# Weights narrowed in seven operations, w_in by halves, w_out inside the loop's first steps, a sign flip moved from GpSimd to ScalarE, and another order of loads, folds and DFT

## Chip, cores, metric

One core of a Trainium2 chip. The metric is the device time of one execution in microseconds (us), the median of several runs. "Span" is the profiled execution's time from the first to the last instruction; it is some 2 us below the run's time.

## The reference

```python
def reference(x, w_in, conv_w, w_out):      # x 8 x 3136 x 256; the weights come as float64
    x = np.fft.fft(np.fft.fft(x, axis=1), axis=2).real.astype(np.float32)
    h = np.maximum(x @ w_in, 0.0)           # w_in 256 x 1024
    conv = sum(conv_w[k] * shift(h, k) for k in range(3))   # along the sequence, zero-padded
    return (h / (1 + np.exp(-conv)) @ w_out).astype(np.float32)   # w_out 1024 x 256
```

The weights arrive as float64, and the kernel computes in fp32 (every matmul of the profile is f32): a "narrowing" takes the two 32-bit words of each float64 apart and builds an fp32 on VectorE.

## The kernel before

A prologue loads everything, narrows the weights, folds the first batch of x (sums and differences of mirrored rows, so that fewer DFT products are needed), multiplies the DFT of the feature axis into w_in (the tile G), and runs the DFT of batch 0 in nine parts. Then 256 steps follow, 32 for each of 8 batches. A step makes two products with G on TensorE, combines them on VectorE, convolves, takes a sigmoid, gates on GpSimd and VectorE, and multiplies by w_out. Folds and DFT of the next batch are "side" work of the steps.

The narrowing of a piece, ten VectorE operations:

```python
ts(out=fi, in0=hi, scalar1=20, scalar2=0x7FF, op0=lsr, op1=ALU.bitwise_and)
ts(out=fi, in0=fi, scalar1=896, scalar2=1151, op0=ALU.max, op1=ALU.min)
ts(out=fi, in0=fi, scalar1=23, scalar2=-0x40000000, op0=lsl, op1=ALU.bitwise_xor)
ts(out=gi, in0=hi, scalar1=-0x80000000, scalar2=None, op0=ALU.bitwise_and)
st(out=fi, in0=fi, scalar=0x7FFFFFFF, in1=gi, op0=ALU.bitwise_and, op1=ALU.bitwise_or)
ts(out=gi, in0=lo, scalar1=1, scalar2=None, op0=lsr)
st(out=g, in0=gi, scalar=2.0 ** -51, in1=f, op0=ALU.mult, op1=ALU.mult)
ts(out=hi_, in0=hi, scalar1=3, scalar2=0x7FFFF8, op0=lsl, op1=ALU.bitwise_and)
tt(out=fi, in0=fi, in1=hi_, op=ALU.bitwise_or)
tt(out=dst, in0=f, in1=g, op=ALU.add)
```

The DFT tables, loaded on SyncE's queue and mended on ScalarE (L198 and L207 to L212):

```python
def load_tables(par):                     # par 1: odd tables, par 0: even tables
    st = slice(2 * par, 2 * par + 2)
    to = tab[:, st].rearrange("p s q i -> p s (q i)")
    for i in range(2):
        nc.sync.dma_start(out=to[i:NP:2], in_=dft_seq[0:NP // 2, st, HQ * i:HQ * (i + 1)]...)  # 49 rows
    nc.sync.dma_start(out=tab[NP:KR, st, HQ - 1], ...)
    nc.sync.dma_start(out=tab[NP:KR, st, 0:HQ - 1], ...)

def mend_tables(par, half):
    row = tab[96:NP, 2 * par:2 * par + 2, HQ - 1]
    act(row, row, AF.Copy, scale=half[96:NP])
    if par:
        for i in range(2):
            for to, of, s in ((4, 3, -1.0), (5, 2, 1.0)):
                act(tab[0:KR, to, :, i:HO:2], tab[0:KR, of, :, i:HO:2], AF.Copy, scale=-s if i else s)
```

The loads of x: in h == 1, eight small "zero-row" loads (the rows that stand for row 0 of each quarter) go to eng2:

```python
def load_ops(b, h, eng, eng2):
    def plain():
        eng.dma_start(out=t[0:NP, 0:4], in_=...)
        if h == 1:
            for s in range(8):
                eng2.dma_start(out=t[NP:KR, s], in_=x[b:b + 1, r * Q4:r * Q4 + 1].to_broadcast([1, 2, D]))
...
for h in range(2):
    for f in load_ops(0, h, nc.sync, nc.scalar):
        f()
```

And the flip, the last operation on the row "er" before it goes out to DRAM and comes back to all partitions, where it seeds a batch's first products:

```python
nc.gpsimd.tensor_scalar(out=t[:, 3:NK:4], in0=t[:, 3:NK:4], scalar1=-1.0, scalar2=None, op0=ALU.mult)
nc.sync.dma_start(out=ed[b:b + 1, :], in_=t)
```

## Time and profile before

| | before |
|---|---|
| median of 3 runs | 1289.94 us |
| span, mean granted clock of TensorE | 1288.0 us, 0.987 |
| start of the first combine (end of the prologue) | 93.06 |
| batch 0 (32 steps) | 154.39 |
| batches 1 to 7, to the end | 1040.55 |

The last three rows sum to the span. They are read from VectorE's timeline: the combine is one VectorE instruction (L492, 512 times in the trace), two of them to a step, so every 64th marks a new batch. Each part of the change touches one of the three stages.

### The profile page before, as it was taken

The numbers are of one execution on the slowest core, as the hardware profiler recorded it, in microseconds if no ns is written. First come the engines' busy times: TensorE is split into PE (matmuls) and PEld (weight loads), VectorE is DVE, ScalarE is ACT, GpSimd is POOL, SyncE is SP. The second block draws the span as 40 slices with busy tenths as digits, with TensorE's granted clock in tenths as the row PEclk, the third lists the DMA queues.
The fourth block names the chain that finished last, engine by engine and source line by source line (L and its number), as shares of the span: only waits on it lengthen the run. The fifth ranks groups of instructions, "written<-read, shape, count | busy, mean of one in ns | idle before, by whom it ended". The sixth has DMA issues, their size and how long they took to land.

```text
span 1288.0 us, 15443 instructions
## 1 busy us (share of the span) xinstructions
PE 1198.0 (93%) x4914; PEld 898.6 (70%) x4914; DVE 1153.2 (90%) x1664; ACT 880.2 (68%) x1814; POOL 404.1 (31%) x507
## 2 busy tenths in 40 slices
PE   0758999999999999999999999999999999999998
PEld 0535677777677766777677776777677777777776
DVE  6869998998989988898899988998999878898996
ACT  0216766777668766777667776777767777777885
POOL 2414524241523334232513225141322213222222
PEclk9868999999999999999999999999999999999999
DMA  7701202020211102020202103020010001100101
GB/s 226 191 26 39 88 26 87 13 78 25 88 38 44 55 30 76 25 78 25 72 29 63 40 25 100 26 77 5 22 50 26 27 25 44 32 6 22 33 26 44
DMA packets 46842, 66.04 MB, mean 51 GB/s; under 512 B 5600, under 2 KB 35196, under 8 KB 46504
## 3 DMA queue, kind: packets, MB, share of 16 engines
q1 hardware_dynamic: 41012, 49.80, 12.5%
q0 software_dynamic: 5120, 12.85, 3.4%
q10 hardware_dynamic: 628, 2.40, 0.6%
q8 instruction: 38, 0.62, 0.2%
q14 instruction: 44, 0.36, 0.1%
HBM read 39.24 MB, written 25.74 MB: 50 GB/s over the span
## 4 chain that ended last, share of the span: by engine, by line
PE 69%; DVE 17%; issue 4%; ACT 4%; DMA 3%; POOL 2%; DVEq 0%; SPq 0%; ACTq 0%; POOLq 0%
PE po L89 43%; PE pb L89 10%; PE pa L89 9%; PE pd L89 7%; DVE g L504 4%; DVE h L492 2%; DVE g L518 2%; ACT nb L481 2%; DMA dm<-dft_dim_dram 1%; POOL er L319 1%; DVE w L174 1%; DVE xh L147 1%; DVE w L175 1%; DVE xh L158 1%; ACT g L510 1%
## 5 line engine op out<-in xcount | busy, mean ns | idle before, releaser
L89 PE MATMUL po<-wout,g 128*128 128x256 f32 (+2 forms) x3200 | 740.1, 381 | 26.6 <-DVE g L518 13.7
L89 PEld LDWEIGHTS po<-wout,g 128*128 128x128 f32 (+2 forms) x3200 | 597.3, 188 | 190.4 <-DVE g L518 43.4
L504 DVE SCALAR_TENSOR_TENSOR g<-h,cw,g 128x770 f32<-128x770 f32 (+2 forms) x512 | 556.9, 1088 | 11.0 <-ACT g L498 1.5
L517 POOL TENSOR_TENSOR g<-g,h 128x385 f32<-128x385 f32 (+1 forms) x256 | 239.5, 937 | 755.2 <-ACT g L510 571.7
L510 ACT ACTIVATE g<-g 128x385 f32<-128x385 f32 (+3 forms) x512 | 244.1, 527 | 187.6 <-DVE g L504 187.3
L481 ACT ACTIVATE nb<-pb 128x386 f32<-128x386 f32 (+4 forms) x512 | 225.5, 494 | 121.8 <-PE pb L89 120.9
L492 DVE CUSTOM_DVE_ANT_0 h<-pa,nb 128x386 f32<-128x386 f32 (+4 forms) x512 | 265.2, 560 | 15.8 <-PE pa L89 10.0
L498 ACT ACTIVATE g<-h,cw 128x770 f32<-128x770 f32 (+2 forms) x256 | 243.7, 952 | 0.0
L89 PE MATMUL pa<-pt,G 128*128 128x386 f32 (+2 forms) x512 | 213.7, 498 | 9.0 <-ACT pa L466 9.0
L89 PE MATMUL pb<-qt,G 127*128 127x386 f32 (+2 forms) x512 | 215.1, 501 | 4.7 <-ACT nb L481 4.7
L518 DVE TENSOR_TENSOR g<-g,h 128x385 f32<-128x385 f32 (+2 forms) x256 | 155.2, 606 | 5.3 <-ACT g L510 5.3
L466 ACT ACTIVATE pa<-eb,ge 128x386 f32<-128x386 f32 (+2 forms) x256 | 153.9, 601 | 8.2 <-DMA eb<-ed 8.0
L89 PEld LDWEIGHTS pa<-pt,G 128*128 128x128 f32 x512 | 97.4, 191 | 83.3 <-issue 19.8
L89 PE MATMUL pd<-tab,w 99*128 99x196 f32 (+2 forms) x448 | 118.6, 374 | 0.0
L89 PEld LDWEIGHTS pb<-qt,G 127*128 127x128 f32 x512 | 94.0, 191 | 32.0 <-ACT nb L481 7.9
L122 POOL DMA_INDIRECT xh<-in_x_dram,idx x64 | 88.0, 1374 | 16.4 <-issue 13.7
L89 PEld LDWEIGHTS pd<-tab,w 99*128 99x128 f32 (+1 forms) x448 | 83.2, 190 | 13.5
L534 ACT COPY os<-po 128x256 f32<-128x256 f32 (+2 forms) x200 | 60.1, 393 | 16.4 <-DMA out_dram<-os 8.6
L89 PE MATMUL po<-win,dm 128*128 128x512 f32 x8 | 6.5, 994 | 39.2 <-DMA dm<-dft_dim_dram 39.2
L147 DVE TENSOR_TENSOR xh<-xh 98x1020 f32<-98x1020 f32 (+1 forms) x32 | 43.0, 1353 | 0.0
L158 DVE TENSOR_TENSOR xh<-xh 98x1024 f32<-98x1024 f32 (+1 forms) x32 | 41.2, 1294 | 0.1
L89 PEld LDWEIGHTS po<-win,dm 128*128 128x128 f32 x8 | 2.5, 330 | 42.3 <-issue 41.3
(84 smaller groups left out, 373.0 us busy)
## 6 DMA issues: line engine op xcount, KB each, us to landing
out_dram<-os SPq DMA_DIRECT2D x184, 128.0 KB
xh<-in_x_dram SPq DMA_DIRECT2D x16, 784.0 KB
eb<-ed SPq DMA_DIRECT2D x16, 193.0 KB
tab<-dft_seq_dram SPq DMA_DIRECT2D x4, 601.8 KB
raw<-in_moe_w_in_dram ACTq DMA_DIRECT2D x2, 1024.0 KB
raw<-in_moe_w_out_dram SPq DMA_DIRECT2D x1, 2048.0 KB
eb<-ed SPq DMA_DIRECT2D x8, 209.0 KB
eb<-ed SPq DMA_DIRECT2D x8, 192.5 KB
```

Source lines behind the costliest of these rows:

```text
L89: nc.tensor.matmul(o, l, r, start=start, stop=stop, skip_group_check=True)
L122: nc.gpsimd.indirect_dma_start(out=xh[b, h][0:NP, 4 + m].rearrange("p q d -> p (q d)"), out_offset=None, in_=bass.AP(tensor=x.tensor, offs ...
L147: vt(a[:, :, :, 1:D], a[:, :, :, 1:D], r[:, :, :, D - 1:0:-1], op=ALU.add)
L466: act(pa[s][:, 0:n], eb[b, c], AF.Copy, scale=ge[:, f:f + 1])
L481: act(nb[s][:, i, cols], p[:, cols], AF.Copy, scale=-1.0 if i else 1.0)
L492: nc.vector._custom_dve(TENSOR_ADD_SAT, out=to, in0=a[:, cols], in1=c[:, i, cols], s0=BIG, s1=0.0)
L498: act(gs[s], hs[s][:, 0:n], AF.Copy, scale=cw[:, 0, s[2]:s[2] + 1])
L504: stt(out=g, in0=h[:, k:k + n], scalar=cw[:, k, f:f + 1], in1=g, op0=ALU.mult, op1=ALU.add)
L510: act(gs[s][:, c], gs[s][:, c], AF.Sigmoid)
L517: gt(g[:, m:n], g[:, m:n], h[:, m + 1:n + 1], op=ALU.mult)
L518: vt(g[:, 0:m], g[:, 0:m], h[:, 1:m + 1], op=ALU.mult)
L534: nc.scalar.copy(out=osb[0:m, j % 2], in_=pt[0:m, j % 2])
```

## The change

The intent: less VectorE work in the prologue (seven operations instead of ten; only half of w_in ahead of the folds, the other half between DFT parts; w_out in the steps 0 to 7), so that the DFT and the steps start earlier, and a GpSimd operation less in each batch. The diff, cut to its core:

```diff
-    def load_ops(b, h, eng, eng2):
+    def load_ops(b, h, eng):
...
-            if h == 1:
-                for s in range(8):
-                    r = s if s < 4 else (8 - s) % 4
-                    eng2.dma_start(out=t[NP:KR, s], in_=x[...].to_broadcast([1, 2, D]))
+        def zero():                      # five loads, on the queue of x
+            for s0, n, r, d in ((0, 4, 0, Q4), (4, 1, 0, Q4), (5, 1, 3, Q4), (6, 1, 2, Q4), (7, 1, 1, Q4)):
+                eng.dma_start(out=t[NP:KR, s0:s0 + n], in_=...)
...
-            return [pair(0), pair(2), both(4, ALU.add), both(6, ALU.subtract), evens, feats(0), feats(1)]
+            return [pair(0), pair(2), both(6, ALU.subtract), feats(1), both(4, ALU.add), evens, feats(0)]
...
-                nc.gpsimd.tensor_scalar(out=t[:, 3:NK:4], ..., scalar1=-1.0, ...)
+        def flip():
+            act(er[b][:, 3:NK:4], er[b][:, 3:NK:4], AF.Copy, scale=-1.0)
...
+        ts(out=d, in0=hi, scalar1=20, scalar2=0x7FF, op0=lsr, op1=ALU.bitwise_and)
+        ts(out=d, in0=d, scalar1=-896, scalar2=0, op0=ALU.add, op1=ALU.max)
+        ts(out=d, in0=d, scalar1=23, scalar2=None, op0=lsl)
+        stt(out=d, in0=hi, scalar=-0x80000000, in1=d, op0=ALU.bitwise_and, op1=ALU.bitwise_or)
+        ts(out=hi, in0=hi, scalar1=0xFFFFF, scalar2=0x100000, op0=ALU.bitwise_and, op1=ALU.bitwise_or)
+        stt(out=lof, in0=lo.bitcast(U32), scalar=2.0 ** -32, in1=hi, op0=ALU.mult, op1=ALU.add)
+        stt(out=dst, in0=lof, scalar=2.0 ** -20, in1=dst, op0=ALU.mult, op1=ALU.mult)
...
+    w_cv.load(nc.scalar)
+    w_in[0].load(nc.scalar, 0)
+    w_in[0].load(nc.sync, 1)
+    for h in range(2):
+        for f in load_ops(0, h, nc.sync):
+            f()
+    nc.scalar.dma_start(out=dm, in_=dft_dim[:, :, 0:2])
+    load_tables(1)
+    for t in range(2):
+        w_in[1].load(nc.sync, t)
+    load_tables(0)
...
+    for i, u in enumerate(us[j] for j in (0, 1, 4, 2, 3, 5, 6, 7, 8)):     # feature part third
+        u.matmuls(0, 1)
+        u.copy()
+        ...                                                                 # row at 1, flip and spread at 2
+        if i in (0, 1, 4, 5):
+            w_in[1].narrow(*quarters.pop(0))
...
+    at(0, "pe", lambda: blocks(1))                    # second half of G
+    for c in range(NF):
+        at(c, "dve", lambda c=c: w_out.narrow(c, slice(0, D)))
...
-    end = 0
+    end = 4
-        stop = per * (b - 1) + max(12 - 4 * (b - 1), 2)
+        stop = per * (b - 1) + max(26 - 8 * b, 2)
```

More of the change, by code (lines that the diff above doesn't have):

```diff
@@ L11 @@
 I32 = mybir.dt.int32
+U32 = mybir.dt.uint32
 AF = mybir.ActivationFunctionType
@@ L113, in plain @@
                 ap=[[HQ * D, NP], [Q4 * D, 4], [1, 2 * D]]))
-            if h == 1:
-                for s in range(8):
-                    r = s if s < 4 else (8 - s) % 4
-                    eng2.dma_start(out=t[NP:KR, s],
-                                   in_=x[b:b + 1, r * Q4:r * Q4 + 1].to_broadcast([1, 2, D]))
+        def zero():
+            t = xh[b, h]
+            for s0, n, r, d in ((0, 4, 0, Q4), (4, 1, 0, Q4), (5, 1, 3, Q4), (6, 1, 2, Q4), (7, 1, 1, Q4)):
+                eng.dma_start(out=t[NP:KR, s0:s0 + n], in_=bass.AP(
+                    tensor=x.tensor, offset=x.offset + (b * S + r * Q4) * D,
+                    ap=[[D, 1], [d * D, n], [0, 2], [1, D]]))
         def mirrored(m):
@@ L129, in mirrored @@
             return f
-        return [plain] + [mirrored(m) for m in range(4)]
+        return [plain] + [zero] * h + [mirrored(m) for m in range(4)]
     def fold_ops(b):
@@ L166, in f @@
                 def f():
-                    if h == 0 and not odd:
-                        wt[b] = wp.tile([P, 8, HQ, P], F32, name="w", tag="w")
+                    if h == 0 and odd:
+                        wt[b] = [wp.tile([P, 4, HQ, P], F32, name="w", tag="w%d" % i) for i in range(2)]
                         ea[b] = ep.tile([P, 2, HQ], F32, name="ea", tag="ea")
-                        nc.gpsimd.memset(wt[b][0:KR, 2:4, :, P - 1:P], 0.0)
-                    w, o, s = wt[b], 4 * odd, 6 * odd
+                        nc.gpsimd.memset(wt[b][0][0:KR, 2:4, :, P - 1:P], 0.0)
+                    w, s = wt[b][odd], 6 * odd
                     v = t()[k, s:s + 2]
                     lo, hi = v[:, :, :, 1:P], v[:, :, :, D - 1:P:-1]
-                    vt(w[k, o:o + 2, qs, 1:P], lo, hi, op=ALU.add)
-                    vt(w[k, o + 2:o + 4, qs, 0:P - 1], lo, hi, op=ALU.subtract)
-                    nc.gpsimd.tensor_copy(w[k, o:o + 2, qs, 0], v[:, :, :, 0])
+                    vt(w[k, 0:2, qs, 1:P], lo, hi, op=ALU.add)
+                    vt(w[k, 2:4, qs, 0:P - 1], lo, hi, op=ALU.subtract)
+                    nc.gpsimd.tensor_copy(w[k, 0:2, qs, 0], v[:, :, :, 0])
                     if odd:
-                        gt(w[k, 6:8, qs, P - 1], t()[k, 7:5:-1, :, P], sg[k], op=ALU.mult)
+                        gt(w[k, 2:4, qs, P - 1], t()[k, 7:5:-1, :, P], sg[k], op=ALU.mult)
                     else:
@@ L181, in feats @@
                 return f
-            return [pair(0), pair(2), both(4, ALU.add), both(6, ALU.subtract), evens,
-                    feats(0), feats(1)]
+            return [pair(0), pair(2), both(6, ALU.subtract), feats(1), both(4, ALU.add), evens,
+                    feats(0)]
         return half(0) + half(1)
@@ L240, in w @@
         def w(i):
-            return lambda k, q: wt[b][0:k, i, q, :]
+            return lambda k, q: wt[b][i // 4][0:k, i % 4, q, :]
         a_ = {}
@@ L318, in fin @@
                     gt(t[:, M - 2 * c:Q4:-4], a[:, 0:nh], bb[:, 0:nh], op=ALU.subtract)
-                nc.gpsimd.tensor_scalar(out=t[:, 3:NK:4], in0=t[:, 3:NK:4], scalar1=-1.0, scalar2=None, op0=ALU.mult)
-                nc.sync.dma_start(out=ed[b:b + 1, :], in_=t)
             return Unit(b, mms, copy, fin)
@@ L328, in row, with store @@
             nc.sync.dma_start(out=er[b], in_=PQ[b][1][P - 1:P, :])
-        return begin, [odd_even(1), odd(1), even(1, 0), even(1, 1), feature(), odd_even(0), odd(0), even(0, 0), even(0, 1)], row
+        def flip():
+            act(er[b][:, 3:NK:4], er[b][:, 3:NK:4], AF.Copy, scale=-1.0)
+        def store():
+            nc.sync.dma_start(out=ed[b:b + 1, :], in_=er[b])
+        return (begin, [odd_even(1), odd(1), even(1, 0), even(1, 1), feature(), odd_even(0), odd(0),
+                        even(0, 0), even(0, 1)], row, flip, store)
     def spread(b):
@@ L363, with narrow @@
     HN = max(c.k1 - c.k0 for c in chunks)
-    def narrow(dst, raw, ng):
-        k, n = dst.shape
-        ts, tt, st = ng.tensor_scalar, ng.tensor_tensor, ng.scalar_tensor_tensor
+    def narrow(dst, raw):
+        ts = nc.vector.tensor_scalar
         lsl, lsr = ALU.logical_shift_left, ALU.logical_shift_right
-        f, g, h = [hp.tile([P, HW], F32, name="nt", tag="h")[0:k, 0:n] for _ in range(3)]
-        fi, gi, hi_ = [t.bitcast(I32) for t in (f, g, h)]
         lo, hi = raw[:, :, 0], raw[:, :, 1]
-        ts(out=fi, in0=hi, scalar1=20, scalar2=0x7FF, op0=lsr, op1=ALU.bitwise_and)
-        ts(out=fi, in0=fi, scalar1=896, scalar2=1151, op0=ALU.max, op1=ALU.min)
-        ts(out=fi, in0=fi, scalar1=23, scalar2=-0x40000000, op0=lsl, op1=ALU.bitwise_xor)
-        ts(out=gi, in0=hi, scalar1=-0x80000000, scalar2=None, op0=ALU.bitwise_and)
-        st(out=fi, in0=fi, scalar=0x7FFFFFFF, in1=gi, op0=ALU.bitwise_and, op1=ALU.bitwise_or)
-        ts(out=gi, in0=lo, scalar1=1, scalar2=None, op0=lsr)
-        st(out=g, in0=gi, scalar=2.0 ** -51, in1=f, op0=ALU.mult, op1=ALU.mult)
-        ts(out=hi_, in0=hi, scalar1=3, scalar2=0x7FFFF8, op0=lsl, op1=ALU.bitwise_and)
-        tt(out=fi, in0=fi, in1=hi_, op=ALU.bitwise_or)
-        tt(out=dst, in0=f, in1=g, op=ALU.add)
@@ L389, in load_weight @@
-    def load_weight(dst, src, ng, eng):
-        k, nc_, n = dst.shape
-        if src.dtype == F32:
-            eng.dma_start(out=dst, in_=src)
-            return []
-        raw = wp.tile([P, nc_ * n, 2], I32, name="raw", tag="w")[0:k]
-        eng.dma_start(out=raw.rearrange("p (c n) e -> p c (n e)", c=nc_), in_=src)
-        to = dst.rearrange("p c n -> p (c n)")
-        w = nc_ * n
-        parts = -(-w // HW)
-        cuts = [slice(w * i // parts, w * (i + 1) // parts) for i in range(parts)]
-        return [(lambda c=c: narrow(to[:, c], raw[:, c], ng)) for c in cuts]
@@ L403, in words @@
-    def words(w):
-        return w if w.dtype == F32 else w.bitcast(I32)
+        lof, d = lo.bitcast(F32), dst.bitcast(I32)
+        ts(out=d, in0=hi, scalar1=20, scalar2=0x7FF, op0=lsr, op1=ALU.bitwise_and)
[3 more added lines that the diff above has]
+        ts(out=hi, in0=hi, scalar1=0xFFFFF, scalar2=0x100000, op0=ALU.bitwise_and, op1=ALU.bitwise_or)
@@ new lines, in narrow, with __init__, load @@
+        stt(out=lof, in0=lo.bitcast(U32), scalar=2.0 ** -32, in1=hi, op0=ALU.mult, op1=ALU.add)
+        stt(out=dst, in0=lof, scalar=2.0 ** -20, in1=dst, op0=ALU.mult, op1=ALU.mult)
+    class Weight:
+        def __init__(self, dst, src, pool, tag):
+            self.dst, self.src = dst, src
+            k, c, n = dst.shape
+            self.raw = None
+            if src.dtype != F32:
+                self.raw = pool.tile([P, c, n, 2], I32, name="raw", tag=tag)[0:k]
+                self.src = src.bitcast(I32)
+        def load(self, eng, c=None):
+            c = slice(0, self.dst.shape[1]) if c is None else slice(c, c + 1)
+            if self.raw is None:
+                eng.dma_start(out=self.dst[:, c], in_=self.src[:, c])
+            else:
+                eng.dma_start(out=self.raw[:, c].rearrange("p c n e -> p c (n e)"), in_=self.src[:, c])
+        def narrow(self, c, cols):
+            if self.raw is not None:
+                narrow(self.dst[:, c, cols], self.raw[:, c, cols])
@@ L413 @@
     nc.gpsimd.tensor_scalar(out=half, in0=half, scalar1=0.5, scalar2=0.5, op0=ALU.mult, op1=ALU.add)
-    wout = const.tile([P, NF, D], F32, name="wout")
-    win = pqp.tile([P, 2, F // 2 + 256], F32, name="win", tag="pt"), pqp.tile([P, 2, F // 2 + 256], F32, name="win", tag="qt")
-    win = [t.rearrange("p a f -> p (a f)")[:, 0:F].unsqueeze(1) for t in win]
-    todo = []
-    for t in range(2):
-        todo += load_weight(win[t], words(moe_w_in)[t * P:(t + 1) * P].unsqueeze(1), nc.vector, nc.scalar)
@@ L420 @@
-    for h in range(2):
-        for f in load_ops(0, h, nc.sync, nc.scalar):
-            f()
-    todo += load_weight(cw24, words(moe_conv_w).rearrange("k (m p) -> (k m) p", m=NF).unsqueeze(1),
-                        nc.vector, nc.scalar)
-    nc.scalar.dma_start(out=dm, in_=dft_dim[:, :, 0:2])
-    for par in (1, 0):
-        load_tables(par)
-    for f in todo:
-        f()
-    late_w = load_weight(wout, words(moe_w_out).rearrange("(c p) o -> p c o", p=P), nc.vector, nc.sync)
-    for par in (1, 0):
-        mend_tables(par, half)
@@ L434 @@
-    G = const.tile([P, 2, F], F32, name="G")
-    for g in range(2):
-        for c in range(0, F, 512):
-            p = psa.tile([P, 512], F32, name="pa", tag="pa") if g else spare()
-            for t in range(2):
-                mm(p, dm[:, t, g, :], win[t][:, 0, c:c + 512], t == 0, t == 1)
-            nc.scalar.copy(out=G[:, g, c:c + 512], in_=p)
-    ge = const.tile([P, NF], F32, name="ge")
-    p = spare()
-    for m in range(NF):
-        for t in range(2):
-            mm(p[:, m:m + 1], win[t][:, 0, m * P:(m + 1) * P], dm[:, t, 1, P - 1:P], t == 0, t == 1)
@@ L447 @@
-    nc.scalar.copy(out=ge, in_=p[:, 0:NF])
-    cw = const.tile([P, 3, NF], F32, name="cw")
-    p = spare()
-    mm(p[:, 0:3 * NF], cw24[:, 0], ident, True, True)
-    nc.scalar.copy(out=cw.rearrange("p k m -> p (k m)"), in_=p[:, 0:3 * NF])
+    H = F // 2
+    win = [pqp.tile([P, NK], F32, name="win", tag=tag)[:, 0:F].rearrange("p (t n) -> p t n", t=2)
+           for tag in ("pt", "qt")]
+    w_cv = Weight(cw24, moe_conv_w.rearrange("k (m p) -> (k m) p", m=NF).unsqueeze(1), gp, "g")
+    w_in = [Weight(win[i], moe_w_in[:, i * H:(i + 1) * H].rearrange("(t p) n -> p t n", p=P), wp, "w%d" % i)
+            for i in range(2)]
@@ new lines @@
+    w_cv.load(nc.scalar)
[9 more added lines that the diff above has]
+    load_tables(0)
+    wout = const.tile([P, NF, D], F32, name="wout")
+    G = const.tile([P, 2, F], F32, name="G")
+    ge = const.tile([P, NF], F32, name="ge")
+    cw = const.tile([P, 3, NF], F32, name="cw")
@@ new lines, in blocks @@
+    def blocks(i):
+        for g in range(2):
+            p = spare() if i else psa.tile([P, 512], F32, name="pa", tag="pa")
+            for t in range(2):
+                mm(p, dm[:, t, g, :], win[i][:, t], t == 0, t == 1)
+            nc.scalar.copy(out=G[:, g, i * H:(i + 1) * H], in_=p)
+        p = spare()
+        for m in range(NF // 2):
+            for t in range(2):
+                mm(p[:, m:m + 1], win[i][:, t, m * P:(m + 1) * P], dm[:, t, 1, P - 1:P], t == 0, t == 1)
+        nc.scalar.copy(out=ge[:, i * NF // 2:(i + 1) * NF // 2], in_=p[:, 0:NF // 2])
@@ L453, with taps @@
+    def taps():
+        p = spare()
+        mm(p[:, 0:3 * NF], cw24[:, 0], ident, True, True)
+        nc.scalar.copy(out=cw.rearrange("p k m -> p (k m)"), in_=p[:, 0:3 * NF])
     rows = out.rearrange("b s d -> (b s) d")
@@ L536, in mm2 @@
         gs.pop(s)
+    w_cv.narrow(0, slice(0, P))
+    for t in range(2):
+        w_in[0].narrow(t, slice(0, H))
     for f in fold_ops(0):
         f()
-    for h in range(2):
-        for f in load_ops(1, h, nc.sync, nc.sync):
-            f()
-    begin, us, row = units(0)
+    w_out = Weight(wout, moe_w_out.rearrange("(c p) o -> p c o", p=P), xp, "xh")
+    w_out.load(nc.sync)
+    taps()
+    blocks(0)
+    for par in (1, 0):
+        mend_tables(par, half)
+    begin, us, row, flip, store = units(0)
     begin()
-    for i, u in enumerate(us):
+    nc.gpsimd.memset(PQ[0][1][96:P, :], 0.0)
+    quarters = [(t, slice(i * H // 2, (i + 1) * H // 2)) for t in range(2) for i in range(2)]
+    for i, u in enumerate(us[j] for j in (0, 1, 4, 2, 3, 5, 6, 7, 8)):
         u.matmuls(0, 1)
         u.copy()
-        if i == 4:
+        if i == 2:
+            flip()
+        u.fin()
+        if i == 1:
             row()
-        u.fin()
-        if i == 4:
+        if i == 2:
+            store()
             spread(0)
-        for g in late_w[i::len(us)]:
-            g()
+            for f in load_ops(1, 0, nc.sync):
+                f()
+        if i in (0, 1, 4, 5):
+            w_in[1].narrow(*quarters.pop(0))
     steps = [(b, c, f) for b in range(B) for c in range(len(chunks)) for f in range(NF)]
@@ L562, in at @@
         side.setdefault((cycle, where), []).append(fn)
+    at(0, "pe", lambda: blocks(1))
+    for c in range(NF):
+        at(c, "dve", lambda c=c: w_out.narrow(c, slice(0, D)))
+    for j, fn in enumerate(load_ops(1, 1, nc.sync)):
+        at(NF + j // 3, "load", fn)
     fold_at, dft_at = {}, {}
-    end = 0
+    end = 4
     for b in range(1, B):
-        stop = per * (b - 1) + max(12 - 4 * (b - 1), 2)
+        stop = per * (b - 1) + max(26 - 8 * b, 2)
         fold_at[b] = (end, stop - end)
@@ L575 @@
         cs = [c0 + j * n // len(ops) for j in range(len(ops))]
+        assert b > 1 or cs[7] > NF + 2
         if b + 1 < B:
@@ L578 @@
                 c1 = cs[7 * h + 6] + 1
-                for j, fn in enumerate(load_ops(b + 1, h, nc.sync, nc.sync)):
+                for j, fn in enumerate(load_ops(b + 1, h, nc.sync)):
                     at(c1 + (j + 1) // 2, "load", fn)
@@ L582 @@
             at(cs[j], "dve", fn)
-        begin, us, row = units(b)
+        begin, us, row, flip, store = units(b)
         c0, n = dft_at[b]
@@ L593 @@
                 at(cs[i + 1], "dve", row)
+                at(cs[i + 1] + 1, "act", flip)
+                at(cs[i + 1] + 2, "load", store)
             at(cs[i + 1], "dve", u.fin)
```

## The prediction

The forecast's sum is 64 + 175 + 1040.5 - 8 = 1271.5 us of span, and 1272 for the median run. In (b), the landing at 39 to 40 is the estimate from the last even table's landing near 40.7.

The trace of the kernel before has these measurements. In a narrowing at 128x512, a tensor_scalar took 422 ns with the strided reads of raw (L377) and 430 on a plain tile (L378), an operation on two tensors 692 (L384). From 21 to 29 us, with almost only tables moving, the DMA share was 0.50 at 181 GB/s. The granted clock was 0.50 from 53.77 us, the start of the DFT, to 58, 0.67 in the next us and 1.00 from 59 to 63; the "first 5 us at half clock" of (c) can be held against that. Its "13 warm" and the DFT's 13.5 of (d) are estimates: at a clock of 1.00, batch 6 with a DFT took 144.0 us, and 32 steps of batch 7 without one come to 129.4 (its 31 pitches, 125.32 us, times 32/31), 14.6 less. ScalarE's 0.5 us for the flip is an estimate too; the trace has its copy of 1x392 at 0.48 us (L309).

> **What bounds the kernel now.** I read, in this order, the page with its 40 slices, the table of busy time by stretch, the timelines of single engines over the first 125 us, the chain of waits, and the DMA bytes by stretch.
>
> ```profile
> PE 1198.0 (93%) x4914; PEld 898.6 (70%) x4914; DVE 1153.2 (90%) x1664; ACT 880.2 (68%) x1814; POOL 404.1 (31%) x507
> ...
> PE   0758999999999999999999999999999999999998
> ...
> DVE  6869998998989988898899988998999878898996
> ```
>
> The table by stretch (start:end, length, then PE, PEld, DVE, ACT, POOL busy with counts, granted clock, DMA share, GB/s) sorts this by stage:
>
> ```profile
> 30.00:40.00 10.00, 0.78 (x1) 0.50 (x2) 7.24 (x16) 2.07 (x2) 0.12 (x1) 1.00 0.81 207
> ...
> 70.00:80.00 10.00, 7.26 (x16) 4.71 (x17) 9.69 (x19) 0.80 (x2) 0.00 (x0) 0.54 0.00 0
> 80.00:90.00 10.00, 2.21 (x11) 1.60 (x10) 2.96 (x8) 0.65 (x2) 4.05 (x8) 0.80 0.07 26
> ...
> 300.00:1200.00 900.00, 880.32 (x3653) 663.89 (x3652) 813.46 (x1169) 655.00 (x1357) 275.45 (x349) 1.00 0.14 42
> ```
>
> From 300 to 1200 us TensorE is busy 880 of 900: nothing that only lightens VectorE pays there. Before the first of the 256 steps stands a prologue. I take the start of the first combine of each batch (32 steps) from VectorE's timeline: 93.06, 247.45, 398.43, 551.03, 701.29, 851.57, 1000.50, 1144.51, end 1288. So the prologue is 93.1 us, batch 0 takes 154.4, the rest 1040.5. The chain of waits shows how the prologue ends (start, length, what):
>
> ```profile
> 79.86 1.91 DMA er<-qt
> ...
> 84.04 1.89 POOL er L319
> ...
> 85.96 1.30 DMA ed<-er
> 87.28 3.32 DMA eb<-ed
> 90.62 0.59 ACT pa L466
> ```
>
> The 10.7 us from 79.86 to seed (90.62) are one row's trip through DRAM and GpSimd while all else has finished (last DFT result at 83.5). Earlier, VectorE narrows w_in and conv_w from 8.2 to 34.9, folds to 52.1, and puts three w_out pieces of some 6.6 us each between the DFT results (57.7 to 79.0). ScalarE's timeline shows a second gate:
>
> ```profile
> 40.78 3.37 ACT L211 ACTIVATE tab<-tab 99x784 f32<-99x784 f32 x4 [8.70 <-DMA tab<-dft_seq_dram]
> ```
>
> The semaphores that this instruction waits for are those of the odd tables and also of the two big transfers of the even tables, the last queued. So the first DFT part (it reads what L211 writes) can't start before both tables have landed, whatever VectorE does.
>
> [...]
>
> ```profile
> L377 DVE TENSOR_SCALAR nt<-raw 128x512 int32<-128x512 int32 x4 | 1.7, 422 | 8.2 <-DMA raw<-in_moe_w_in_dram 8.2
> ...
> L384 DVE SCALAR_TENSOR_TENSOR nt<-nt 128x512 f32<-128x512 int32 x4 | 2.8, 692 | 0.1
> ```
>
> [...]
>
> **The change part by part.**
>
> (a) Narrowing: six tensor_scalar and four two-tensor operations become four and three. Ten cost 5.3 us at 512 columns, 6.6 at 682 and 2.4 at 128 (timeline), hence about 1.45 us fixed and 7.5 ns a column. Seven: slope 4 x 0.53 + 3 x 1.05 = 5.3 ns (0.17 us over 170 columns for each tensor_scalar, 0.18 for each two-tensor one), fixed about 1.05 us. So 3.8 us at 512, 2.4 at 256. Ahead of the folds remain conv_w and half of w_in: 1.7 + 2 x 3.8 = 9.3 us instead of 24. With 1 MB of w_in to land first (about 6 us) the 17.2 us of folds end near 32 us, not 52.
>
> (b) Loads. [...] That landed near 40.7 before. Only the order changes (half of w_in between the tables), so I keep 39 to 40; w_out follows the tables again and shares their end. L211 then needs 3.4 us: the DFT starts at about 43 instead of 53.8. VectorE idles from 32 to 43; this is where most of gain (a) is lost.
>
> (c) From DFT start to first combine, before: 93.06 - 53.77 = 39.3 us. New: TensorE needs about 16 us for the nine parts (13 warm, the first 5 us at half clock); VectorE has 5.7 us of DFT results and 4 quarters x 2.4 = 9.8 us, starting 2.5 us in, so 18 to 19 us in all with one or two short waits. The row now starts after the second part and the feature part is third: at about 50.5, er 1.9, flip on ScalarE 0.5, GpSimd's four additions 2.2, ed 1.3, eb 3.3 to 4.5 beside the x loads: seed near 61. Last result near 62.5, then one product and the combine: first step at about 64 (before 93.1): **29 saved**.
>
> (d) Steps 0 to 7 take w_out: 8 x 2.4 = 19.5 us on VectorE. A step with no side work is 3.4 us on VectorE (its fastest pitch); a fold adds 1.23. Steps 0 to 11 were VectorE-bound: 12 x 3.4 + 14.7 = 55.5, measured 55.7. New: folds go to steps 4 to 17, so the first 18 steps are VectorE-bound: 18 x 3.4 + 17.2 + 19.5 = 98, plus 1 to 2 for the second half of G, which TensorE does at step 0 (about 7 us, delaying products of step 2). Steps 18 to 31 are TensorE-bound: 3.89 a step of six tiles, 4.43 of seven (pitches of batch 7), DFT 13.5, so 6 x 3.89 + 8 x 4.43 + 13.5 = 72, plus the 3 to 4 by which this sum misses steps 12 to 31 of before (98.7). Batch 0: about 175 against 154.4: **20.5 lost**.
>
> (e) The flip of er leaves GpSimd. In each of batches 1 to 6 TensorE stands still once because the gate's GpSimd half waits behind L319:
>
> ```profile
> 482.69 2.64 POOL L319 TENSOR_SCALAR er<-er 1x392 f32<-1x392 f32 x1
> 485.23 0.86 POOL L517 TENSOR_TENSOR g<-g,h 128x385 f32<-128x385 f32 x1
> ```
>
> ```profile
> 486.14 1.56 PE L89 MATMUL po<-wout,g 128*128 128x256 f32 x6 [2.06 <-POOL g L517]
> ```
>
> TensorE's idle times at these places are 1.8, 2.1, 2.0, 2.0, 1.5 and 0.9 us, 10.4 in all. ScalarE does it in some 0.5 us (a 1x392 copy) with 32% of its time free. I count **8 saved**.
>
> Sum of the span: 64 + 175 + 1040.5 - 8 = 1271.5. The median run is 1.9 us over the traced span (1289.9 against 1288.0): 1273, and I say 1272.
>
> **Rivals.**
> 1. *The tables do not gate.* Early half-weights leave room and the tables land by 30 us, or L211 waits for the odd one alone. Then the DFT starts at about 29 (folds) and the first step at 50 to 52: 1258 to 1260. Against it: [...] L211's semaphores.
> 2. *The moved narrowing costs all it saves.* If [...] the fold of the second half of x (loaded only from step 8, after raw w_out is free; gathers took 8.4 us to land) stalls VectorE at step 11, batch 0 takes 185: 1282. For it: the fold comes only about three steps after the load. [...]
> 3. *VectorE-bound steps leave slack that hides it.* If TensorE makes up after step 18 (the DFT in ten steps is dense), the loss is 16 rather than 20: 1268.
> 4. *ScalarE's flip blocks.* It waits in order for a row that took 1.9 to 4.7 us to land; should seeds slip, (e) gives nothing: 1280.
>
> **Range and chances.** First step 64 +-6, batch 0 175 +-6, the later batches -8 +-4: as independent errors about +-9.5, so 1259 to 1285. Faster by over 2% means under 1264.1, which needs most of rival 1 or two favourable errors: 0.18. Slower by over 2% needs a new stall in every batch: 0.01.
>
> **What would show each step.** Narrowing groups: seven a piece, 128x256 at 0.30 (tensor_scalar) and 0.42 us. L211's start (39 to 40) and VectorE idle ahead of it; if it starts by 30, (b) is wrong. First combine at 58 to 70. Combine pitches of 5.9 to 7.1 in steps 2 to 7; batch 0 at 175. No TensorE gap over 1 us behind GpSimd's gate in batches 1 to 6; batch 1 on about as long as before less 1 to 2 each. The prediction is wrong if the second half of x makes VectorE wait, or the DFT of batch 1 in ten steps lets TensorE wait for its one PSUM bank.

## More of the kernel before

On SyncE's queue of the kernel before (start, length until the next issue, issuing line, what, how many):

```profile
0.74 0.90 SPq L111 DMA_DIRECT2D xh<-in_x_dram  x2
1.68 12.93 SPq L198 DMA_DIRECT2D tab<-dft_seq_dram  x2
```

and on ScalarE's queue, the same view:

```profile
1.68 25.04 ACTq L117 DMA_DIRECT2D xh<-in_x_dram  x8
```

The first table transfer leaves SyncE at 1.68, right behind x. The eight zero-row loads hold ScalarE's queue for 25 us. Issuing one takes 0.57 us (median), so eight account for some 5 us; the rest they wait for something, and whatever stands behind them waits too (conv_w's load leaves at 26.82).

## The result, and the profile after

The changed kernel is correct and takes 1280.31 us against 1290.42 in the same rounds. That is the median of four runs; one of them took 1423.89 us at a mean clock of 0.843, a slow run, which is used nowhere else. The three fast runs are 1278.58, 1279.88 and 1280.73 us. Ratios in this document are the mean time of one kernel's fast runs over that of the other's of the same rounds, so not quite the ratio of the quoted medians: here 0.9916, 95% interval 0.9896 to 0.9935. The change makes the kernel 0.84% faster, within 2%.

| us | before | predicted | after |
|---|---|---|---|
| start of the first combine | 93.06 | 64 | 73.31 |
| batch 0 | 154.39 | 175 | 174.72 |
| batches 1 to 7 | 1040.55 | 1032.5 | 1031.0 |
| span | 1288.0 | 1271.5 | 1279.0 |

Against before: 19.8 us won in the prologue, 20.3 lost in batch 0, 9.6 won later. Against the prediction: one stage is off, the prologue, by 9.3 us.

The page after, busy time and two rows of slices:

```profile
PE 1196.6 (94%) x4914; PEld 898.0 (70%) x4914; DVE 1145.5 (90%) x1689; ACT 884.4 (69%) x1823; POOL 398.5 (31%) x500
...
PE   2487899999999999999999999999999999999998
...
DVE  7399999999999898998999888998999888898996
```

TensorE now works in the first two slices (32 us each): the first half of G is done before the DFT. VectorE's second slice has fallen from 8 to 3 tenths: it waits there for the tables, as shown below. The stretches after, with the columns explained in the prediction:

```profile
30.00:40.00 10.00, 0.99 (x2) 0.50 (x2) 5.47 (x8) 0.95 (x1) 4.02 (x5) 0.50 0.74 194
41.00:48.00 7.00, 0.00 (x0) 0.00 (x0) 0.00 (x0) 0.00 (x0) 0.00 (x0) 0.50 0.84 191
70.00:80.00 10.00, 8.00 (x23) 4.43 (x23) 8.48 (x24) 4.16 (x8) 0.00 (x0) 0.83 0.49 132
...
300.00:1200.00 900.00, 887.21 (x3690) 671.27 (x3689) 817.33 (x1181) 665.48 (x1376) 271.23 (x345) 1.00 0.13 42
```

From 41 to 48 us not one engine computes; only transfers run. At 70 to 80 us, where before the DFT of batch 0 was still under way, the steps have begun. In the long stretch TensorE is busy 887 of 900 us, 7 more than before; e1 and e11 below tie this to the flip, gain (e).

The chain of waits after, from 24 us to the first combine (start, length, what):

```profile
25.88 22.21 DMA tab<-dft_seq_dram
48.24 3.24 ACT tab L215 x4
51.52 2.34 PE po L90 x6
...
58.54 1.90 DMA er<-qt
...
62.33 0.57 POOL er L322
62.93 0.33 ACT as L258
...
73.31 1.02 DVE h L505 x2
```

One even table's transfer, issued by 25.88 and landed at 48.09, ends everybody's wait. Then come the mending on ScalarE (L215), the first DFT part, and from there mostly VectorE's mix of DFT results and quarters of w_in. The first leg of the row's trip is still on the chain: from 58.54 to 62.9 the row lands and GpSimd makes its sums (L321, L322), and only then does ScalarE copy the next DFT part (L258), for which VectorE waits 0.65 us. The second leg, through DRAM to the seed, which ended the prologue before, is off it: the first seed now runs at 68.90, before VectorE's last DFT result at 71.69. The mending on ScalarE's timeline, to be held against the one of before that the prediction shows:

```profile
48.24 3.23 ACT L215 ACTIVATE tab<-tab 99x784 f32<-99x784 f32 x4 [13.36 <-DMA tab<-dft_seq_dram]
```

It starts at 48.24, 7.5 us later than in the kernel before, though the folds now end at 35.6 and no longer at 52.1. What VectorE pays, on its timeline after:

```profile
54.24 0.36 DVE L281 TENSOR_TENSOR as<-as,po 128x196 f32<-128x196 f32 x1 [18.67 <-ACT as L277]
```

It idles 18.67 us ahead of its first DFT result. And the reason, on SyncE's queue after (columns as before):

```profile
2.15 18.79 SPq L120 DMA_DIRECT2D xh<-in_x_dram  x5
20.98 1.67 SPq L202 DMA_DIRECT2D tab<-dft_seq_dram  x2
...
24.98 1.68 SPq L202 DMA_DIRECT2D tab<-dft_seq_dram  x2
```

The zero-row loads (L120, five now) have moved from ScalarE's queue to SyncE's, ahead of the tables, and hold it for 18.79 us. The first table transfer leaves at 20.98 instead of 1.68. The chain puts their wait down to a transfer of x that landed at 20.36; why loads of a few KB have to wait for it, no run shows.

### The profile page after: what moved, and what is told of

It is laid out like the page before. It is cut to its first block, busy times and chain, and to the rows that moved or that the text cites. A ratio compares the mean times of both kernels' runs of the same rounds, so it can differ in the third digit from the quotient of the medians.

```text
span 1279.0 us, 15442 instructions
## 1 busy us (share of the span) xinstructions
PE 1196.6 (94%) x4914; PEld 898.0 (70%) x4914; DVE 1145.5 (90%) x1689; ACT 884.4 (69%) x1823; POOL 398.5 (31%) x500
## 4 chain that ended last, share of the span: by engine, by line
PE 66%; DVE 16%; DMA 6%; issue 5%; ACT 5%; POOL 2%; SPq 1%; DVEq 0%; ACTq 0%; POOLq 0%
PE po L90 41%; PE pb L90 10%; PE pa L90 9%; PE pd L90 7%; DVE g L517 4%; DVE h L505 2%; DVE g L531 2%; DMA xh<-in_x_dram 2%; ACT nb L494 2%; DMA tab<-dft_seq_dram 2%; DMA out_dram<-os 2%; DVE xh L151 1%; ACT g L523 1%; DVE xh L162 1%; POOL xh L126 1%
## 5 line engine op out<-in xcount | busy, mean ns | idle before, releaser
L530 POOL TENSOR_TENSOR g<-g,h 128x385 f32<-128x385 f32 (+1 forms) x256 | 243.9, 954 | 760.6 <-ACT g L523 569.2
L126 POOL DMA_INDIRECT xh<-in_x_dram,idx x64 | 96.4, 1506 | 18.1 <-issue 12.0
L90 PEld LDWEIGHTS pd<-tab,w 99*128 99x128 f32 (+1 forms) x448 | 83.0, 190 | 13.6
L90 PE MATMUL po<-tab,w 98*128 98x196 f32 (+4 forms) x64 | 16.6, 420 | 26.3 <-ACT tab L215 15.6
L90 PEld LDWEIGHTS po<-tab,w 98*128 98x128 f32 (+1 forms) x64 | 12.8, 215 | 29.6 <-ACT tab L215 16.1
```

The lines of the kernel that those rows point to most:

```text
L90: nc.tensor.matmul(o, l, r, start=start, stop=stop, skip_group_check=True)
L126: nc.gpsimd.indirect_dma_start(out=xh[b, h][0:NP, 4 + m].rearrange("p q d -> p (q d)"), out_offset=None, in_=bass.AP(tensor=x.tensor, offs ...
L530: gt(g[:, m:n], g[:, m:n], h[:, m + 1:n + 1], op=ALU.mult)
```

## The experiments

Twelve kernels, each on one chip beside the kernel before; all gave correct results. The table gathers the three stages of each profiled execution; ratio is to the kernel before in the same rounds. "Mend" is the start of the four-instruction mending of the tables. The changed kernel was timed in a call of its own, so kernels of different calls are compared by their ratios and by the stages, not by their medians.

| kernel | mend | first combine | batch 0 | rest | median | ratio [95%] |
|---|---|---|---|---|---|---|
| after | 48.24 | 73.31 | 174.72 | 1031.0 | 1280.31 | 0.9916 [0.9896, 0.9935] |
| e1_flip_gpsimd | | 73.74 | 181.03 | 1040.7 | 1296.05 | 1.0040 [1.0015, 1.0066] |
| e2_tables_48_rows | 39.38 | 65.30 | 174.59 | 1031.7 | 1272.42 | 0.9866 [0.9846, 0.9885] |
| e3_own_tables | 34.65 | 66.13 | 174.54 | 1030.0 | 1273.57 | 0.9878 [0.9858, 0.9897] |
| e4_w_in_after_tables | 43.20 | 68.72 | 175.05 | 1030.5 | 1276.22 | 0.9895 [0.9875, 0.9914] |
| e5_ten_operations | | 77.31 | 182.55 | 1030.0 | 1292.04 | 1.0030 [1.0014, 1.0047] |
| e6_w_out_in_dft | | 93.94 | 161.54 | 1030.1 | 1287.16 | 0.9991 [0.9974, 1.0008] |
| e7_quarters_early | | 70.94 | 174.47 | 1029.7 | 1277.35 | 0.9919 [0.9902, 0.9935] |
| e8_all | 27.38 | 56.47 | 174.91 | 1030.7 | 1263.64 | 0.9809 [0.9793, 0.9825] |
| e9_zero_act | 45.34 | 70.40 | 174.96 | 1030.0 | 1277.63 | 0.9900 [0.9882, 0.9918] |
| e10_zero_act_w_in_after | 36.89 | 63.07 | 174.52 | 1029.8 | 1269.17 | 0.9835 [0.9819, 0.9852] |
| e11_before_flip_scalar | | 90.21 | 152.82 | 1031.9 | 1276.79 | 0.9895 [0.9879, 0.9912] |
| e12_before_seven | | 85.59 | 154.41 | 1041.4 | 1283.39 | 0.9946 [0.9929, 0.9962] |

Five kernels' times fell outside what was expected: e1 (1296.05 for 1286 to 1289), e5 (1292.04 for 1288 to 1291) and e6 (1287.16 for 1278 to 1284) were slower, e10 (1269.17 for 1272 to 1274) and e11 (1276.79 for 1279 to 1281) faster. e2 and e3 came 2.4 and 2.6 us above what was said to be "about".

The first group asks why the tables came late; the theory is that the transfers' order, width and shared wait set the mending's start, and the rival that something else on ScalarE or VectorE does.

**e4: the second half of w_in behind both tables.**

```diff
     load_tables(1)
+    load_tables(0)
     for t in range(2):
         w_in[1].load(nc.sync, t)
-    load_tables(0)
```

> The changed kernel with the second half of w_in queued behind the even tables instead of between the tables. Theory: [...] they land 3 to 5 us earlier (43 to 45), and the first combine comes 3 to 5 us earlier: 1275 to 1278. Rival: the table engines are slow because other transfers run beside them, whatever the order: within 1.5 us of the changed kernel.

By ScalarE's timeline the mending starts at 43.20, 5.0 us earlier, still ended by a table transfer, and the first combine comes 4.6 earlier. So the megabyte of w_in between the tables is on the path, and taking it out is worth about half of the 9.3 us.

**e9: the zero rows of batch 0 back on ScalarE's queue.**

```diff
-                eng.dma_start(out=t[NP:KR, s0:s0 + n], in_=bass.AP(
+                (eng if b else nc.scalar).dma_start(out=t[NP:KR, s0:s0 + n], in_=bass.AP(
...
+    nc.scalar.dma_start(out=dm, in_=dft_dim[:, :, 0:2])      # moved ahead of the loads of x
     for h in range(2):
```

> The changed kernel with the five zero-row loads of batch 0 on ScalarE's queue (dm issued ahead of them), so that the sync queue issues the tables early instead of at 21 us. Theory: the sync queue stands 18.8 us behind these loads, and the DMA engines run dry for about 2 us before the first table: tables land 2 to 3 us earlier (45 to 46), first combine at 70 to 71.5, time 1277 to 1278. Rival: the tables stood behind x in the engines anyway: within 1 us of the changed kernel.

The mending starts 2.9 us earlier, at 45.34, and the first combine comes 2.9 earlier. Alone it is the smaller part: SyncE's queue now issues the tables early but stands still a second time, ahead of a small table transfer, until 23.85, and w_in is still between the tables.

**e10: e9 and e4 together.**

```diff
+    (e9)
     load_tables(1)
+    load_tables(0)
     for t in range(2):
         w_in[1].load(nc.sync, t)
-    load_tables(0)
```

> Both: zero-row loads on ScalarE's queue and the second half of w_in behind the tables. Theory: these two, the order and the held queue, are all of what my predicted landing of the tables (39 to 40) missed: tables land at 40 to 41.5, first combine at 65 to 67, time 1272 to 1274. Rival: one of them shadows the other: 1275 to 1277, as with w_in behind the tables alone.

ScalarE's timeline:

```profile
36.89 3.23 ACT L215 ACTIVATE tab<-tab 99x784 f32<-99x784 f32 x4 [8.66 <-DMA tab<-dft_seq_dram]
```

Together they bring 11.4 us at the mending, more than the sum of 5.0 and 2.9. Undoing these two restores what the prediction had assumed, and more: 36.89 against the predicted 39 to 40, and a first combine at 63.07 against the predicted 64. The stretch from 21 to 24 us shows how, first after, then e10:

```profile
21.00:24.00 3.00, 3.00 (x20) 2.25 (x18) 2.97 (x4) 0.59 (x1) 1.31 (x2) 1.00 0.22 51
```

```profile
21.00:24.00 3.00, 3.00 (x12) 1.68 (x11) 2.97 (x4) 1.61 (x3) 1.31 (x2) 1.00 0.44 180
```

In the changed kernel the DMA engines are nearly idle there (share 0.22, 51 GB/s; from 20 to 22 us it is 0.01 or less): x has landed and the tables have only just been issued. In e10 the tables are being moved at 180 GB/s with a DMA share of 0.44, as much as 7 of the 16 engines busy throughout (an estimate: 0.44 x 16 = 7.0).

**e2: tables in 48 rows and a rest of one row.** In the changed kernel the DMA share is 0.45 from 24 to 26 us, as much as 7 of the 16 engines (an estimate: 0.45 x 16 = 7.2). That 48 rows in place of 49 would use all 16 was the supposition.

```diff
         for i in range(2):
-            nc.sync.dma_start(out=to[i:NP:2], in_=dft_seq[0:NP // 2, st, HQ * i:HQ * (i + 1)]
+            nc.sync.dma_start(out=to[i:96:2], in_=dft_seq[0:48, st, HQ * i:HQ * (i + 1)]
                               .rearrange("p s q i -> p s (q i)"))
+        nc.sync.dma_start(out=to[96:NP], in_=dft_seq[48, st].rearrange("s (i q) k -> i s (q k)", i=2))
```

> The changed kernel with each big table transfer as 48 partitions (and the last row pair apart) in place of 49. Theory: the DFT starts late (51.5) because four transfers of 600 KB cross only 7 of 16 DMA engines: with 16 engines the tables land about 10 us earlier (near 38), the first combine at 63 to 65 in place of 73.3, time about 1270. Rival: the bytes as a whole or the waits of the issuing queue set the landing: tables land at 45 or later and the time stays at 1276 or more.

By ScalarE's timeline the mending starts at 39.38, 8.9 us earlier, with every byte and its order unchanged: from 24 to 26 us the DMA share is 1.02, against 0.45 in the changed kernel. So the transfers of 49 rows, which left over half of the DMA engines' time unused in that stretch, are a bottleneck of the prologue. First combine 8.0 us earlier.

**e3: odd and even tables in tiles of their own.** If L215 waits for the even tables only because they share a tile with the odd ones, it should start at the odd ones' landing.

```diff
-    tab = const.tile([P, 6, HQ, HE], F32, name="tab")
+    tabs = [const.tile([P, 2 + 2 * i, HQ, HE], F32, name="tab%d" % i) for i in range(2)]
...
-    for par in (1, 0):
-        mend_tables(par, half)
+    mend_tables(1, half)
...
     for i, u in enumerate(...):
+        if i == 2:
+            mend_tables(0, half)
```

> The changed kernel with odd and even tables in tiles of their own, so that the odd parts wait for odd tables alone, and the even row mended just before the feature part. Theory: the wait for the even tables is what holds the DFT: the first part then starts at 37 to 39 in place of 51.5, and as the feature part still waits for the even tables (48) the first combine comes at 63 to 66: time about 1271. Rival: the DFT waits for the odd tables or the folds anyway: start at 48 or later, time 1278 or more.

ScalarE's timeline:

```profile
33.67 0.95 ACT L212 ACTIVATE tab<-tab,half 2x786 f32<-2x786 f32 x1 [9.44 <-DMA tab<-dft_seq_dram]
34.65 3.26 ACT L216 ACTIVATE tab<-tab 99x784 f32<-99x784 f32 x4
47.20 0.94 ACT L212 ACTIVATE tab<-tab,half 2x786 f32<-2x786 f32 x1 [6.54 <-DMA tab<-dft_seq_dram]
```

The mending of the odd tables starts 13.6 us earlier, without a wait for a transfer of its own, and only the third part, which needs the even tables, waits until 47.20. So L215's wait for the even tables came from the shared tile and not from its operands. But the first combine moves only 7.2 us: the wait goes to the next part.

**e7: the four quarters of the second half of w_in narrowed ahead of the mending.** VectorE idles for 18.67 us; this puts its 10 us of quarters there.

```diff
     blocks(0)
+    for a_q in quarters:
+        w_in[1].narrow(*a_q)
     for par in (1, 0):
         mend_tables(par, half)
...
-        if i in (0, 1, 4, 5):
-            w_in[1].narrow(*quarters.pop(0))
```

> The changed kernel with the four pieces of the second half of w_in narrowed right after the folds, where VectorE idles 18.7 us for the tables. Theory: DFT start stays at 51.5; what follows it is then bound by TensorE instead of VectorE, first combine at 69.5 to 71.5: time 1277 to 1278.5. Rival: TensorE sets the pace of the DFT already: within 1 us of the changed kernel.

By the times it can't be told from the changed kernel (0.9919 and 0.9916). In the trace the first combine comes 2.4 us earlier. So of the quarters' 10 us only about 2.4 had been on the path; the path has another limit of nearly the same length: in e7 the chain runs from the mending through TensorE's DFT, 18.12 us without a break.

**e8: e2, e3 and e9 together, with the halves of w_in's first half narrowed in the order in which they land.**

```diff
+    (e2, e3, e9)
-    for t in range(2):
+    for t in (1, 0):
         w_in[0].narrow(t, slice(0, H))
```

> Tables of their own in transfers of 48 partitions, zero-row loads of batch 0 on ScalarE's queue (so that the sync queue is not held), the first-landed piece of w_in narrowed first, even row mended before the feature part. Theory: nothing but VectorE is then left ahead of the DFT: folds end at 32, DFT starts at 30 to 35, first combine at 51 to 56, time 1258 to 1264: faster than both kernels. Rival: another transfer takes the place of the tables (x, or er and eb behind w_out): first combine at 60 or later, time 1267 or more.

ScalarE's timeline, then TensorE's:

```profile
27.38 3.33 ACT L217 ACTIVATE tab<-tab 99x784 f32<-99x784 f32 x4
```

```profile
31.23 6.38 PE L90 MATMUL po<-tab,w 99*128 99x196 f32 x16 [6.92 <-POOL w L182]
```

The DFT starts at 31.23: the tables no longer gate, GpSimd's last piece of the folds does. The first combine is at 56.47, and the kernel takes 1263.64 us (1263.20 to 1264.18): faster than both, by 1.9% against the kernel before (at the 2% line the verdict is unclear, 0.9793 to 0.9825). What each of its four parts gives is not told apart. With the gate gone, rival 1 of the prediction happens, though its first step comes at 56.5, not 50 to 52.

The second group undoes the other parts.

**e1: the flip back on GpSimd.**

```diff
                     gt(t[:, M - 2 * c:Q4:-4], a[:, 0:nh], bb[:, 0:nh], op=ALU.subtract)
+                nc.gpsimd.tensor_scalar(out=t[:, 3:NK:4], in0=t[:, 3:NK:4], scalar1=-1.0, scalar2=None, op0=ALU.mult)
...
-            act(er[b][:, 3:NK:4], er[b][:, 3:NK:4], AF.Copy, scale=-1.0)
+            pass
```

> The changed kernel with the sign flip of er back on GpSimd (ScalarE's flip left out). Theory: the flip was worth about 8 us in batches 1 to 6, by the 1 to 2 us that TensorE stood behind GpSimd's gate in each: time about 1286 to 1289, with TensorE gaps of 1 to 2 us behind the gate again. Rival: batches 1 to 7 got shorter by the other spread of folds, loads and DFT: then within 3 us of the changed kernel (1280). The first combine stays within 3 us of 73.3 in both.

**e11: the kernel before with only the flip moved to ScalarE.**

```diff
-                nc.gpsimd.tensor_scalar(out=t[:, 3:NK:4], ..., scalar1=-1.0, scalar2=None, op0=ALU.mult)
-                nc.sync.dma_start(out=ed[b:b + 1, :], in_=t)
+        def flip():
+            act(er[b][:, 3:NK:4], er[b][:, 3:NK:4], AF.Copy, scale=-1.0)
+        def store():
+            nc.sync.dma_start(out=ed[b:b + 1, :], in_=er[b])
...
+                at(cs[i + 1] + 1, "act", flip)
+                at(cs[i + 1] + 2, "load", store)
```

> The kernel before with one part of the change alone: er's sign flip on ScalarE, with its store two steps later. Theory: TensorE's stops behind GpSimd's gate vanish in batches 1 to 6 there too: batches 1 to 7 together 8 to 10 us shorter (1040.5 to 1031 or so), prologue 1 us shorter, time 1279 to 1281. Rival: it needs the new spread of folds and DFT: 1286 or more.

TensorE's waits on GpSimd's gate from batch 1 on (who waits, for whom, us in total, times, longest), before, after, e1 and e11:

```profile
PE po L89 <- POOL g L517: 11.6, 9, 2.1
```

```profile
PE po L90 <- POOL g L530: 2.8, 6, 0.7
```

```profile
PE po L90 <- POOL g L531: 9.4, 7, 2.1
```

```profile
PE po L89 <- POOL g L521: 2.8, 6, 0.7
```

In these four kernels the wait goes with the flip: 11.6 and 9.4 us where GpSimd does it, 2.8 where ScalarE does. The batches after the first follow: 1040.55 and 1040.7 against 1031.0 and 1031.9.

In e1 batch 0 is longer by 6.3 us too, nearly all of it in two steps, 25 and 26 (8.9 and 8.3 us, against 4.5 and 6.9 after). TensorE's timeline in e1 shows where that begins:

```profile
210.41 2.93 PE L90 MATMUL po<-wout,g 128*128 128x256 f32 x6 [3.05 <-POOL g L531]
```

The flip runs on GpSimd from 205.12 for 2.33 us, the gate's half stands behind it, and TensorE behind that for 3.05 us. The stretch after it, in e1 and then in the changed kernel:

```profile
212.00:229.50 17.50, 17.11 (x60) 11.89 (x58) 10.47 (x18) 8.10 (x19) 1.96 (x2) 0.87 0.12 43
```

```profile
212.00:229.50 17.50, 17.02 (x74) 13.34 (x73) 14.76 (x25) 13.35 (x30) 4.23 (x6) 1.00 0.19 64
```

TensorE is as busy in both, but at a granted clock of 0.87 instead of 1.00 and with 60 matmuls instead of 74: in this execution the stretch behind the stall ran at the lower clock too; that the stall lowered it is not shown. It may vary from run to run: e1's fastest run took 1292.46 us at a mean clock of 0.982, the profiled one 1297.34 at 0.977. In e11 the prologue also gains, 2.9 us, since there the flip stood on the row's trip to the seed. The outcome for the whole is plain: **the flip alone, in the kernel before, gives 1276.79 us, at least as much as the whole change (ratios 0.9895 and 0.9916, their intervals overlap); and the change without it is slower than the kernel before** (by 0.4%).

**e12: the kernel before with only the seven-operation narrowing.**

```diff
-        f, g, h = [hp.tile(...)]        # and the ten operations
+        lof, d = lo.bitcast(F32), dst.bitcast(I32)
+        # the seven operations of the change, in place
```

> The kernel before with the seven-operation narrowing alone. Theory: conv_w's landing (32.4) hides what w_in saves, so the folds start less than 1 us earlier; the three w_out pieces between the DFT parts fall from 6.6 to 4.7 us each: first combine at 86 to 88 in place of 93.1, time 1283 to 1285. Rival: the DFT is bound by TensorE there and hides it: 1288 or more.

The prologue is 7.5 us shorter, the other stages the same within 0.9. The cheaper narrowing is a gain by itself.

**e5: three operations added to each narrowing of at most 256 columns**, two tensor_scalar and one scalar_tensor_tensor into a scratch tile that nobody reads.

```diff
         stt(out=dst, in0=lof, scalar=2.0 ** -20, in1=dst, op0=ALU.mult, op1=ALU.mult)
+        if n > 256:
+            return
+        g = scr[0:k, 0:n].bitcast(I32)
+        ts(out=g, in0=hi, scalar1=20, scalar2=0x7FF, op0=lsr, op1=ALU.bitwise_and)
+        ts(out=g, in0=g, scalar1=896, scalar2=1151, op0=ALU.max, op1=ALU.min)
+        stt(out=g, in0=hi, scalar=-0x80000000, in1=g, op0=ALU.bitwise_and, op1=ALU.bitwise_or)
```

> The changed kernel with three dead operations (two of one source, one of two) added to every narrowing of 256 columns, so ten there again; results as before. Theory: each 256-column piece costs 0.9 to 1.0 us more; the eight of w_out lie in steps that VectorE bounds, so +7 to +8 in batch 0, and the four of w_in lie between DFT parts, +1 to +3.5: time 1288 to 1291, that is, the seven-operation form is worth about all that the change gained. Rival: steps 0 to 7 have slack that hides it: 1283 or less.

Batch 0 grows by 7.8 us and the prologue by 4.0. The eight pieces of w_out get some 0.29 + 0.29 + 0.43 = 1.0 us of operations each, so 8.1: VectorE-bound steps pay the added work in full, or nearly.

**e6: w_out narrowed between the DFT parts instead of in the steps.**

```diff
+        if i < NF:
+            w_out.narrow(i, slice(0, D))
...
-    for c in range(NF):
-        at(c, "dve", lambda c=c: w_out.narrow(c, slice(0, D)))
```

> The changed kernel with w_out narrowed between the DFT parts (one of its eight pieces after each of the first eight) in place of steps 0 to 7. Theory: the work is VectorE's bound in either place, so it is moved, not removed: first combine at 88 to 92 in place of 73.3, batch 0 at 156 to 160 in place of 174.7, time 1278 to 1284. Rival: the steps hide it: time 1290 or more.

The prologue grows by 20.6 us, batch 0 shrinks by 13.2 only. This was expected to come out even and did not, and it is not a clean undo: the second half of G, which TensorE makes at step 0, now stands exposed (TensorE's timeline):

```profile
96.15 4.09 PE L90 MATMUL po<-win,dm 128*128 128x512 f32 x8
100.08 1.84 PE L90 MATMUL po<-dm,win 128*128 128x1 f32 x16
```

Step 1 takes 7.0 us for these 5.9 us of TensorE work, while VectorE has no side work in steps 0 to 3 (the folds stay at steps 4 to 17). In the changed kernel the same work lies beside the narrowing of w_out. So taking w_out out of the steps uncovers the second half of G: in step 1 VectorE waits 3.96 us for TensorE. That is part of the 7.4 us by which the two stages don't balance; the rest was not traced. The steps are the better place for w_out: the ratio is 0.9991 with w_out between the DFT parts, 0.9916 with it in the steps, with intervals well apart.

## Why the prediction was right or wrong

**The class and the range were right**: 1280.3 lies in 1259 to 1285, within 2%. The middle was 8 us low, and one step of the sum made it so. The prologue missed its own range (first combine at 58 to 70); the total stayed in its range because the other two stages came within 1.5 us. The stated range is wider than the +-9.5 that the prediction works out for it, but 1280.3 lies in that too.

**(a) Narrowing: right.** The groups after, by form, in 54 to 73 us (line, engine, operation, shapes, count, busy us, mean ns, idle before):

```profile
L392 DVE SCALAR_TENSOR_TENSOR win<-raw,win 128x256 f32<-128x256 f32 x4 | 2.0, 510 | 0.1
...
L390 DVE TENSOR_SCALAR raw<-raw 128x256 int32<-128x256 int32 x4 | 1.2, 296 | 0.1
...
L385 DVE TENSOR_SCALAR win<-raw 128x256 int32<-128x256 int32 x4 | 1.1, 285 | 0.0
```

Four tensor_scalar at some 0.29 us and three two-tensor operations at 0.43 to 0.51 give 2.5 us for 256 columns (2.4 predicted); in the trace a piece takes some 2.6 with its gaps. The in-place operation on stride-2 words (L390) took 296 ns, against 285 for the one that writes a plain tile (L385), so slower operations of this kind did not come. Two slips of the working cost nothing: a tensor_scalar grows by 0.09 us over 170 columns (0.53 ns each, as the sum has it), not 0.17, and steps 0 to 11 before took 55.9, not 55.7. The folds ended at 35.6 instead of 32, because the first half of w_in landed at 10.1 rather than 6 (VectorE waited 4.40 us for it); the late tables hid that.

**(b) Loads: wrong, and this is the mis-sized term.** The prediction kept the tables' landing at 39 to 40 with the words "Only the order changes (half of w_in between the tables)". It landed at 48.1; the mending started at 48.24, the DFT at 51.5 rather than 43, the first combine at 73.3 rather than 64. Of the 9.3 us, 8.7 are here (48.24 against 39.5): from the mending's start to the first combine the prediction had about 24.5 us and the trace has 25.1. Two things were read wrongly in the diff and the profile before:

1. *An order on a queue that waits is not "only the order".* The same bytes move, but they start later. The queue with the zero rows stood for 25 us in the kernel before, ScalarE's, where the tables did not follow it. The change puts those rows on SyncE's queue ahead of the tables, and from 20 to 22 us the DMA engines stand idle (share 0.01 or less). The diff's removed argument eng2 said so.
2. *w_in's second half is between the tables*, on the path. The prediction named the new place and kept w_in's bytes in its count, as if they cost the same there as at the very start, where the kernel before has them.

e9 puts 2.9 us on the first, e4 5.0 on the second, e10 11.4 on both; the predicted 64 then comes as 63.07. The two together bring 3.4 us more than their sum, and no run shows why. The traces give a hint. In e10 from 21 to 24 us, with hardly anything but tables moving, 180 GB/s go at a DMA share of 0.44; in the changed kernel from 38 to 41 us, with w_out (issued at 34.70) beside the even tables, 223 GB/s go at a share of 1.05. By an estimate from these shares of 16 engines, a busy engine moves 26 GB/s in the first stretch (180 / (0.44 x 16)) and 14 in the second (223 / 16). The rate isn't the same in both, so a count of bytes at one rate, as the prediction made it, can't give the landing. No run takes the 2 MB of w_out out of the tables' way, so its part in the late landing stays untested. What else made the tables a gate: their 49 rows (e2, 8.9 us) and the wait for the even tables in L215 (e3, 13.6 us at the mending). The prediction knew of both; neither is a part of the change.

**(c) From the DFT's start to the first combine: right**, 21.8 us against 21. The flip took 0.92 us on ScalarE rather than 0.5. The seed was on time; VectorE waited 0.38 and 0.65 us for ScalarE's copies behind the row. The slow start at half clock came much as said: the granted clock is 0.50 from 51.5 to 54 us, 0.65 from 54 to 56, and 1.00 from 56 to 65.

**(d) w_out in the steps: right.** 174.72 against 175, and not by luck: the first 18 steps take 98.4 us (99 to 100 predicted), the rest 76.3 (75 to 76). Steps 2 to 7 take 6.0 to 7.3 us (5.9 to 7.1 predicted). Rival 2's stall did not come: steps 11 and 12, where the second half of x is folded, take 4.6 and 5.4 us, and between 100 and 250 us VectorE waits for no transfer. Rival 3 (slack in the steps hides the narrowing) would have given a shorter batch 0 than 175; that did not happen, and e6 agrees with the small term of 1 to 2 us for the second half of G: it is mostly hidden as long as the narrowing of w_out lies beside it.

**(e) The flip: right**, 9.6 us won against 8; e1 and e11 tie it to the flip. Rival 4 (ScalarE's flip blocks) is false.

**Where the expected gain went.** The reordering won 19.8 us in the prologue, 9 less than predicted, for the tables came late; batch 0 gave 20.3 back, since the 19.5 us of w_out stand in VectorE-bound steps. What is left over is the flip's gain in the later batches, 9.6 us here and 8.7 in e11. None of it was lost to contention in the long stretch, which gained.

## What to carry to other kernels

When a diff moves a load to another queue, look in the trace of before at what that queue and that load wait for: here five loads of at most 8 KB held SyncE's queue for 18.79 us, and the tables issued behind them left it at 20.98 instead of 1.68. Work moved from a prologue into steps is a gain only where those steps have slack on the engine that does it; here they had hardly any, and the two large terms cancelled (19.8 us won, 20.3 lost). A short operation can weigh more than its length where the busiest engine's work queues behind it: the flip, 2.6 us of GpSimd in each batch (1.91 to 2.70) and 0.9 on ScalarE (0.91 to 0.94), was worth as much as the whole change.
